# ScalarE's copies of the first phase of a fused SSM-convolution and gated-MLP gradient kernel: program order, and one deferrable copy per row block

## The chip, the core and the metric

The kernel runs on one core of a Trainium2 chip. A core has TensorE (matmuls, transposes; results go to PSUM), VectorE, ScalarE, GpSimd and SyncE, each with its own instruction stream in an order that is fixed when the kernel is built. SyncE, GpSimd and ScalarE also issue DMA transfers. The metric is device time in microseconds (us). The profiled execution is a single one, taken by the hardware profiler.

## The reference: what is computed

With S = 2048 rows, D = 1024 columns, F = 3584, all in bf16 at the edges:

```python
xn = layernorm(A_q)
k_shift = sum of four shifted copies of A_k times shift_k
kv = k_shift * A_v
y = irfft(rfft(kv padded to 2S) * rfft(ssm_k padded to 2S))[:S] + kv * ssm_D
s = xn * y
g = silu(((xn @ w_gate) * (xn @ w_up)) @ w_down)
out = A_q + s * g
```

The outputs are `out` and the gradients of all nine inputs for a given `grad_out`.

## The kernel before

**Phases.** In the first phase (about 31 to 505 us, with a start before it) TensorE computes the gate and up products. `F` is cut in 14 slabs of 256 columns (`wslab`, two buffers, loaded on SyncE's queue); the 2048 rows are 16 blocks of 128. A *row block*, or row, is one pass of `gu_unit`'s inner loop: eight matmuls of 128x512 (L671) into a PSUM tile `psg` (two buffers), then a ScalarE copy (L673, the *eviction*) to `gut` in SBUF. There are 14 x 16 = 224 rows; they are numbered 1 to 224 in order, and "eviction n" is that of row n. Four rows make a unit: its `gut` is stored to DRAM by a DMA on ScalarE's queue (L72), VectorE multiplies its halves to `hN` (three buffers, stored to `Hd` on GpSimd's queue), and of two units of `hN` 32 half transposes (`turn_pair`) make a PSUM tile `tr`, which two ScalarE copies (L705) bring to `hT`. `hT` has one buffer; SyncE stores it to `HTd` (L706), and the next pair's first copy must wait until that store has read it. `tr` has one buffer, which the filter transposes share.

Beside this, VectorE and TensorE run the forward long convolution, one step at a time, from a generator (`conv_forward`) that `tick` advances after each row. It handles eight blocks `ds` of 128 channels. For each one:

- the filter rows come from DRAM (`load_h`, GpSimd's queue, into half of `U5`), four ScalarE *quarter copies* reorder them into `hx` (L785, 128x512 each, read at a stride of eight elements), 32 half transposes turn them in `tr` (called at L807; the profile shows the helper's line, L565, for these and for those of `hN`), and two *back copies* bring them to `hx` again (L809);
- TensorE makes spectra in `psF` (PSUM, two buffers), and ScalarE copies them to `SP` (L256, L295; two buffers of two copies), which VectorE reads;
- VectorE sums, multiplies spectra and sums again; TensorE transforms back (`psI`, L455) and ScalarE copies to `yf` (L825).

For the first filter block TensorE transposes directly and two ScalarE copies scale into `hx` (L802). `turn_tables` makes the inverse tables `TI` by two copies of 128x2048 (L193).

After the first phase come the down product, the gating, and the backward products and convolutions, to 1914 us.

**What sets the order.** A planner orders each engine's instructions by its own estimate of when each is ready, with the program's order as priority. `keep_in_program_order` takes that freedom from an instruction: it stays behind all that was written before it on its engine. Before the change this holds for VectorE's steps (`tt`, `stt`) and the first matmul of each spectrum of `cmm`, not for ScalarE's copies. In the program, the four quarter copies stand at the first four steps of the spectral product and the turn at the fifth; both copies of a pair follow its transposes at once:

```python
for n, w in enumerate(product(KX, HX, KX, cs, False, 0)):
    if n < 4:
        h_order(ds + 1, n)
    else:
        h_turn(ds + 1)
    yield w
```

`pe_us` and `net` make a step of the convolution cheaper by the TensorE time that it added, so that the generator keeps pace with the rows.

Of the kernel before, what the change touches and what calls it, by code (L numbers as in the profile page):

```python
# [19 lines left out]
def build_kernel(  # L20
# [39 lines left out]
    def ld(out, in_):  # L60
        return nc.sync.dma_start(out=out, in_=in_)
# [9 lines left out]
    def sta(out, in_):  # L71
        return nc.scalar.dma_start(out=out, in_=in_)  # L72
# [113 lines left out]
    def turn_tables(psp):  # L186

        for j in range(2):
            ps = psp.tile([P, 8, 2, P], BF16, name="psT", tag="psF")
            for r in range(8):  # L190
                for k in range(2):
                    nc.tensor.transpose(ps[:, r, k, :], T4[j][:, r, k, :], ident[:])
            nc.scalar.copy(out=TI[:, j], in_=ps[:])  # L193
            yield


# [32 lines left out]
    def cmm(ps, T, x, rs, first=None, held=False):  # L229

        xr = x.rearrange("p (c r) d -> p r c d", c=2)
        for k in range(2):
# [5 lines left out]
            if first is not None and k == 0:  # L238
                nc.tensor.matmul(ps[:, 0, 0:P], T[:, 0, 0, :], first, start=False, stop=True)

    pe_us = [0.0]

    def net(w):
# [4 lines left out]
    def fwd4_half(x, i, wp, psp, first=None):  # L248

        pe_us[0] += 1.75  # L250
        SP = wp.tile([P, 2, 2, 512], F32, name="SP", bufs=2)
        for par in range(2):
            ps = psp.tile([P, 2, 2, 256], F32, name="psF")
            cmm(ps[:, 0], T4[par], x, (i, i + 4), first if i == 0 else None, True)
            cmm(ps[:, 1], T4[par], x, (i + 2, i + 6))
            nc.scalar.copy(out=SP[:, :, par], in_=ps[:].rearrange("p s k x -> p s (k x)"))  # L256
        return SP

    def fwd4_buf(wp):
# [27 lines left out]
    def fwd8_half(x, i, SP, psp, first=None, held=False):  # L287

        pe_us[0] += 0.87
        for j in range(2):  # L290
            r = 2 * i + j
            ps = psp.tile([P, 2, 2, 256], F32, name="psF")
            cmm(ps[:, 0], T4[0], x, (r,), first if r == 0 else None, held)
            cmm(ps[:, 1], T4[0], x, (r + 4,))
            nc.scalar.copy(out=SP[:, :, j], in_=ps[:].rearrange("p s k x -> p s (k x)"))  # L295

    def fwd8(SPs, X, W, C, ahead, late=False):

# [262 lines left out]
    def turn_halves(ps, src):  # L561

        for hh in range(2):
            rows = slice(64 * hh, 64 * hh + 64)
            ins = nc.tensor.transpose(ps(hh), src[rows], ident[rows, rows])  # L565
        return ins

    def halves(x):
        return x.rearrange("p b (h u) -> p h b u", h=2)
# [64 lines left out]
    later = []  # L634
    gu_mm = [None]

    def tr_tile():
        return ps_tr.tile([P, 2, 8, P], BF16, name="tr")

    def defer(fn):  # L640
# [14 lines left out]
    def gu_unit(sl, b0, n, w, tick):  # L655
# [11 lines left out]
        for i in range(n):  # L667
            q, qi = divmod(b0 + i, 4)
            ps = ps_gu.tile([P, 512], F32, name="psg")
            for dc in range(DC):  # L670
                gu_mm[0] = nc.tensor.matmul(ps[:], XNT[q][:, dc, qi * P:(qi + 1) * P],  # L671
                                            w[:, dc].rearrange("p a f -> p (a f)"), start=(dc == 0), stop=(dc == DC - 1))
            nc.scalar.copy(out=gut[:, :, i], in_=ps[:].rearrange("p (a f) -> p a f", a=2))  # L673
            flush(5)
            if i == 0:
                turn_late()
            hn[0]()
            hn[0] = nop
            tick()
        sta(GUd[sl, b0 // 8][:, :, b0 % 8:b0 % 8 + n], gut[:, :, 0:n])  # L680

        def multiply():
# [24 lines left out]

        def store(hT):
            half, rest = divmod(b0, 8)
# [30 lines left out]
    def conv_forward():  # L740
# [12 lines left out]
        def load_h(ds):  # L753
            hrow = U[5][:, 0:2048].rearrange("p (c u r) -> p c u r", c=2, r=8)
            cld(U[5][:, 0:2048], A_ssm_k[ds * P:(ds + 1) * P, :])
            S_["h", ds] = hrow
# [18 lines left out]
            yield 2.3  # L775

        def h_order(ds, part):
            if ds == 8:
                return
            hrow = S_["h", ds]  # L780
            if part == 0:
                S_["hx"] = cf.tile([P, NB, P], BF16, name="hx")
            if ds > 0:
                c, q = divmod(part, 2)
                nc.scalar.activation(S_["hx"][:, 4 * part:4 * part + 4, :], hrow[:, c, :, 4 * q:4 * q + 4].rearrange("p u r -> p r u"),  # L785
                                     ACT.Copy, scale=WSC)
                if part == 3 and ds + 1 < 8:
                    load_h(ds + 1)

        def h_turn(ds):  # L790
            if ds == 8:
                return
            hx = S_["hx"]
            pe_us[0] += 0.67
            if ds == 0:
                hrow = S_["h", 0]
                ps = tr_tile()
                for b in range(NB):
                    with tc.issue_after(tr_ln[0].ins) if b == 0 else nullcontext():
                        nc.tensor.transpose(ps[:, b // 8, b % 8, :], hrow[:, b // 8, :, b % 8], ident[:])  # L800
                    if b % 8 == 7:
                        nc.scalar.activation(hx[:, b - 7:b + 1, :], ps[:, b // 8], ACT.Copy, scale=WSC)  # L802
                load_h(1)
            else:
                ps = tr_tile()[:].rearrange("p h b x -> p h (b x)").rearrange("p h (b u) -> p h b u", u=64)
                for b in range(NB):
                    turn_halves(lambda hh: ps[:, hh, b], hx[:, b, :])  # L807
                for c in range(2):
                    nc.scalar.copy(out=halves(hx[:, 8 * c:8 * c + 8, :]), in_=ps[:, :, 8 * c:8 * c + 8])  # L809
            h_out.append(ds)  # L810

        def kvs(ds):
            return S_["kvt", ds // 2][:, :, ds % 2 * P:(ds % 2 + 1) * P]
# [1 line left out]
        def tail(ds):  # L815
            G = S_.pop(("G", ds))
            if ds < 7:
                yf = cs.tile([P, NB, P], BF16, name="yf")[:]
            else:
                yf = krow[:].rearrange("p a b d -> p (a b d)")[:, 0:NB * P].rearrange("p (b d) -> p b d", b=NB)  # L820
            for rq in range(2):
                ps = (ps_tr if cv_gone else ps_cv).tile([P, 4, 256], F32, name="psI", tag="tr" if cv_gone else "psF")
                inv_quad(G, ps, rq, ds in INV8)
                pe_us[0] += 0.9 if ds in INV8 else 1.8
                nc.scalar.copy(out=yf.rearrange("p (c r) d -> p r c d", c=2)[:, 4 * rq:4 * rq + 4], in_=rowps(ps))  # L825
# [50 lines left out]
        yield from shift(0)  # L876
        PIN[0] = True
        yield 3.9
        h_order(0, 0)
        h_turn(0)  # L880
        yield 0.1
        tl = turn_tables(ps_cv)
        sp = [half(0, S_["hx"], i, Dz[:, 0:P]) for i in range(2)]
        for ds in range(8):
# [11 lines left out]
            if ds == 0:  # L896
                yield from transform(0, 1, sp, HX, own_room(KX), lambda i: sph.append(half(0, kvs(0), i)), nop)
            else:
                yield from transform(ds, 0, sp, KX, own_room(HX), lambda i: sph.append(half(ds, S_["hx"], i, D0)), nop)
                S_["kst"] = st(KFd[ds], KX[:])  # L900
            calls = []

# [13 lines left out]
                S_["filters"] = False  # L916
            st(HFd[ds], HX[:])
            for n, w in enumerate(product(KX, HX, KX, cs, False, 0)):
                if n < 4:
                    h_order(ds + 1, n)  # L920
                else:
# [80 lines left out]
    def tick(by=1):  # L1002
        cnt[0] += by
        if cnt[0] == -4:
            pump((SHIFT_W + 4.05) / F_TOTAL)
        if cnt[0] >= -2:
            pump((SHIFT_W + (F_TOTAL - SHIFT_W) * (cnt[0] + 6.5) / (NT + 3.5)) / F_TOTAL)
# [60 lines left out]
    pss = [ps_bm.tile([P, D], F32, name="psbm") for i in range(2)]  # L1068
    with tc.issue_after(bm_first(range(4)).ins):
        flush()  # L1070
    for p_ in (ps_gu, fg, fw):
        p_.release()
    ub = pool("ub", 1, side="right")
# [752 lines left out]
```

## Time and profile before

| what | value |
|---|---|
| median of 3 runs | 1915.73 us (1915.4 to 1916.0) |
| profiled execution, its time | 1915.55 us |
| its span, first to last instruction | 1913.8 us |
| granted TensorE clock | 1.00 in all slices |
| first phase, 31 to 505 us: TensorE / VectorE / ScalarE busy | 463.15 / 462.48 / 307.15 us of 474 |
| eviction (L673), 128x512 | 0.59 us |
| spectra, back and `hT` copies, 1024 elements | 1.02 us |
| quarter copy (L785), 128x512 at a stride | 1.17 us |
| copy of `TI` (L193), 2048 elements | 1.86 us |

The profile gives each instruction its line in the kernel, its output and input tiles, its start and its duration. A number in square brackets in a timeline is the engine's idle time just ahead of the instruction, with what ended it. A matmul is shown for 0.38 us although the next may follow earlier, so TensorE counts as busy a little beyond what it issues. PE is TensorE, DVE VectorE, ACT ScalarE, SP SyncE; "ACTq" and "SPq" are the queues' DMA issues.

### The profile page before, as it was taken

Reading aid. Unit: us, or ns where it says so; the run is one execution under the profiler, and the core shown is the slowest. Engines: PE = TensorE matmul, PEld = TensorE weight load, DVE = VectorE, ACT = ScalarE, POOL = GpSimd, SP = SyncE. Lnnn points to the kernel's source line nnn. Section 1 sums busy time; section 2 is a strip of 40 time slices with the busy share of each in tenths; the row PEclk is TensorE's granted clock in tenths of the full one; section 3 lists DMA queues with packets and bytes.
Section 4 is the critical chain, followed back from the end, with each engine's and each line's share of the span. In section 5 each row is a group of like instructions: output and inputs, shape, how many; then the busy total and the mean of one; then the engine's idle time right before and its main releaser. Section 6 shows DMA issues by size and latency. Waiting matters only on the chain.

```text
span 1913.8 us, 28261 instructions
## 1 busy us (share of the span) xinstructions
PE 1890.4 (99%) x11350; PEld 1007.9 (53%) x11491; DVE 1550.6 (81%) x1711; ACT 664.0 (35%) x955; POOL 332.8 (17%) x465
## 2 busy tenths in 40 slices
PE   8999999999999999999999999999999999999999
PEld 5555555545544456666666665664444444444444
DVE  8999999999978556887999999999995205788862
ACT  5765666656433233432222222222222102110121
POOL 5121211201103220001031221111212101111120
PEclk9999999999999999999999999999999999999999
DMA  8777766769769997677887698585887999989862
GB/s 292 273 240 235 259 219 219 234 224 298 249 207 301 326 321 231 209 238 230 273 266 262 223 265 265 182 286 177 226 246 171 228 201 196 186 183 190 187 181 89
DMA packets 425107, 444.35 MB, mean 232 GB/s; under 512 B 268400, under 2 KB 342796, under 8 KB 410512
## 3 DMA queue, kind: packets, MB, share of 16 engines
q1 hardware_dynamic: 367504, 239.03, 46.4%
q0 software_dynamic: 41152, 174.15, 28.9%
q10 hardware_dynamic: 16320, 29.36, 4.1%
q8 instruction: 90, 1.47, 0.3%
q14 instruction: 41, 0.34, 0.1%
HBM read 193.87 MB, written 189.84 MB: 200 GB/s over the span
## 4 chain that ended last, share of the span: by engine, by line
PE 94%; DVE 2%; ACT 2%; issue 1%; DMA 0%; SPq 0%; ACTq 0%
PE psb L1517 20%; PE psx L1662 20%; PE psg L671 17%; PE psb L1500 10%; PE psbm L1052 10%; PE psb L1600 9%; PE psF L234 3%; PE tr L565 1%; PE psI L455 1%; DVE W L212 1%; ACT hx L785 1%; PE psY L1211 1%; PE psY L445 1%; PE psx L1600 1%; DVE bst L578 0%
## 5 line engine op out<-in xcount | busy, mean ns | idle before, releaser
L671 PE MATMUL psg<-wslab,U 128*128 128x512 bf16 x1727 | 398.0, 380 | 12.2 <-ACT gut L673 3.8
L1517 PE MATMUL psb<-U,U 128*128 128x512 bf16 x1792 | 397.1, 379 | 0.0
L1662 PE MATMUL psx<-U,dgut 128*128 128x512 bf16 x1505 | 331.0, 379 | 1.6
L1662 PEld LDWEIGHTS <-dgut 128*128 128x128 bf16 x1792 | 174.9, 98 | 211.8
L1517 PEld LDWEIGHTS <-U 128*128 128x128 bf16 x1792 | 174.9, 98 | 198.3
L671 PEld LDWEIGHTS <-U 128*128 128x128 bf16 x1792 | 172.0, 98 | 203.8 <-issue 9.8
L1500 PE MATMUL psb<-wdt,U 128*128 128x256 bf16 x1792 | 205.6, 273 | 0.0
L1500 PEld LDWEIGHTS <-U 128*128 128x128 bf16 x1792 | 174.8, 98 | 29.6
L212 DVE TENSOR_TENSOR W<-W 128x1024 f32<-128x1024 f32 (+1 forms) x189 | 186.5, 1003 | 4.0
L1600 PE MATMUL psb<-U,U 128*128 128x512 bf16 x797 | 176.1, 380 | 0.9
L1522 ACT CAST wb<-psb 128x512 bf16<-128x512 f32 x112 | 65.7, 587 | 315.3 <-PE psb L1517 307.5
L1267 DVE SCALAR_TENSOR_TENSOR dkp<-dkT,kT 128x1024 bf16<-128x1024 bf16 (+2 forms) x64 | 78.3, 1224 | 94.5 <-DMA dkT<-DKSHd 92.8
L1052 PE MATMUL psbm<-U,ht 128*128 128x512 bf16 x658 | 145.1, 379 | 0.7
L1600 PEld LDWEIGHTS <-U 128*128 128x128 bf16 x896 | 87.2, 98 | 104.5
L1694 ACT ACTIVATE dx_t<-dxn 128x1024 bf16<-128x1024 f32 x15 | 15.9, 1057 | 324.9 <-DVE dxn L212 320.1
L673 ACT CAST gut<-psg 128x512 bf16<-128x512 f32 x156 | 91.4, 592 | 101.9 <-PE psg L671 96.3
L1052 PEld LDWEIGHTS <-ht 128*128 128x128 bf16 x672 | 65.5, 98 | 78.3
L212 DVE TENSOR_TENSOR U<-U,dht 128x2048 bf16<-128x2048 bf16 x56 | 68.3, 1221 | 46.7 <-ACT dht L1502 46.7
L1502 ACT CAST dht<-psb 128x512 bf16<-128x512 f32 x112 | 65.7, 588 | 116.1 <-PE psb L1500 115.0
L66 POOL DMA_DIRECT2D Hd<-hN x54 | 37.1, 687 | 256.8 <-DVE hN L212 254.0
L1641 ACT CAST wbs<-psb 128x512 bf16<-128x512 f32 x51 | 29.9, 587 | 145.4 <-PE psb L1600 134.4
L212 DVE TENSOR_TENSOR W<-SP 128x1024 f32<-128x1024 f32 x64 | 74.3, 1219 | 1.5 <-ACT SP L295 0.8
(265 smaller groups left out, 2361.0 us busy)
## 6 DMA issues: line engine op xcount, KB each, us to landing
U<-GUd SPq DMA_DIRECT2D x28, 1024.0 KB, 9.2
DGd<-U SPq DMA_DIRECT2D x28, 1024.0 KB, 5.9
GUd<-gut ACTq DMA_DIRECT2D x39, 512.0 KB, 6.5
out_dram<-wb SPq DMA_DIRECT2D x112, 128.0 KB, 4.4
U<-Hd SPq DMA_DIRECT2D x14, 1024.0 KB, 5.9
Hd<-hN POOLq DMA_DIRECT2D x54, 256.0 KB, 4.4
HTd<-hT SPq DMA_DIRECT2D x24, 512.0 KB, 4.0
ht<-HTd SPq DMA_DIRECT2D x18, 512.0 KB, 7.8
```

Of the source, the lines that this page charges most:

```text
L212: pinned(V.tensor_tensor(o, a, b, op))
L234: mm = nc.tensor.matmul(ps[:, k].rearrange("p (c d) -> p c d", c=2), T[:, r, k, :], xr[:, r], start=(n == 0), stop=(n == len(rs) - 1 and ( ...
L671: gu_mm[0] = nc.tensor.matmul(ps[:], XNT[q][:, dc, qi * P:(qi + 1) * P], w[:, dc].rearrange("p a f -> p (a f)"), start=(dc == 0), stop=(dc ...
L673: nc.scalar.copy(out=gut[:, :, i], in_=ps[:].rearrange("p (a f) -> p a f", a=2))
L1052: mm = nc.tensor.matmul(ps[:, dh * 512:(dh + 1) * 512], ht(fc)[:, i * P:(i + 1) * P], WD[fc // 4][:, fc % 4, dh * 512:(dh + 1) * 512], sta ...
L1267: ins = V.scalar_tensor_tensor(prod[:].rearrange("p r d -> p (r d)")[:, lo:H], dkT[:, 0, lo:H], 1.0, kT[:, 0, 13 + m + lo:13 + m + H], op0 ...
L1500: nc.tensor.matmul(ps[:, x * SLW:(x + 1) * SLW], DBMT[2 * hf + g][:, dc, (b % 4) * P:(b % 4 + 1) * P], wdt[:, dc, :], start=(dc == 0), sto ...
L1502: nc.scalar.copy(out=dht[:, 2 * e:2 * e + 2].rearrange("p b f -> p (b f)"), in_=ps[:])
L1517: nc.tensor.matmul(ps[:], XN[b // 4][:, b % 4, dc * P:(dc + 1) * P], dgus[b // 8][:, :, b % 8], start=(b == 0), stop=(b == NB - 1))
L1522: nc.scalar.copy(out=wb[:, dc % 2].rearrange("p a f -> p (a f)"), in_=ps[:])
L1600: nc.tensor.matmul(ps, h[:, f, b, :], DBM[b // 4][:, b % 4, dh * 512:(dh + 1) * 512], start=(b == 0), stop=(b == NB - 1))
L1662: nc.tensor.matmul(ps[:, dh * 512:(dh + 1) * 512], t[n][:, f, i * P:(i + 1) * P], WGU[n][:, f, dh * 512:(dh + 1) * 512], start=(n == 0 and ...
```

## The change

Every ScalarE copy of the first phase that follows the start of the convolution (`PIN[0]`) is held in program order by `copied`; the pairs' and filters' deferrable copies too. These are no longer written where they arise. They go to a list, `slow`: four quarter copies, the turn and two back copies of a filter block at its end; the two copies of an `hT` at its head. `act_us` is a running account of ScalarE's work: `one_tick` takes 2.0 us off it for each row and adds 0.6 for the eviction, and each copy adds its cost. After each row `run_slow` takes entries while the account stays below 2.2. `tr_tile`, which hands out the single `tr` tile, first takes entries until the tile's copies are out; `hx(ds)` does so until the filter is there.

```diff
+    act_us = [0.0]
+    slow = []
+
+    def copied(us, ins=None):
+        act_us[0] += us
+        if ins is not None and PIN[0]:
+            tc.keep_in_program_order(ins)
+
+    def one_tick():
+        act_us[0] = max(0.0, act_us[0] - 2.0) + 0.6
+
+    def run_slow(all_=False):
+
+        while slow and (all_ or act_us[0] + slow[0][0] < 2.2):
+            us, fn = slow.pop(0)
+            copied(us)
+            fn()
...
-            nc.scalar.copy(out=SP[:, :, par], in_=ps[:].rearrange("p s k x -> p s (k x)"))
+            copied(1.0, nc.scalar.copy(out=SP[:, :, par], in_=ps[:].rearrange("p s k x -> p s (k x)")))
...
+    tr_held = []
+
     def tr_tile():
+        while tr_held:
+            slow.pop(0)[1]()
         return ps_tr.tile([P, 2, 8, P], BF16, name="tr")
...
-            nc.scalar.copy(out=gut[:, :, i], in_=ps[:].rearrange("p (a f) -> p a f", a=2))
+            one_tick()
+            copied(0.0, nc.scalar.copy(out=gut[:, :, i], in_=ps[:].rearrange("p (a f) -> p a f", a=2)))
...
             tick()
+            run_slow()
...
-            for g in range(2):
-                nc.scalar.copy(out=halves(hT[:, 2 * g:2 * g + 2].rearrange("p q a i s -> p (q a i) s")), in_=ps[:, :, 8 * g:8 * g + 8])
-            ht_st[0] = ld(to.rearrange("q f a s -> f q (a s)"), hT[:].rearrange("f q a i s -> f q (a i s)"))
+
+            def copy(g):
+                copied(0.0, nc.scalar.copy(out=halves(hT[:, 2 * g:2 * g + 2].rearrange("p q a i s -> p (q a i) s")),
+                                           in_=ps[:, :, 8 * g:8 * g + 8]))
+                if g == 1:
+                    tr_held.clear()
+                    ht_st[0] = ld(to.rearrange("q f a s -> f q (a s)"), hT[:].rearrange("f q a i s -> f q (a i s)"))
+            tr_held.append(True)
+            slow.insert(0, (1.0, lambda: copy(1)))
+            slow.insert(0, (1.0, lambda: copy(0)))
...
+        def h_back(ds, c):
+            copied(0.0, nc.scalar.copy(out=halves(S_["hx"][:, 8 * c:8 * c + 8, :]), in_=S_["hps"][:, :, 8 * c:8 * c + 8]))
+            if c == 1:
+                tr_held.clear()
+                h_out.append(ds)
+
+        def h_rows(ds):
+            if ds < 8:
+                pe_us[0] += 0.67
+                for part in range(4):
+                    slow.append((1.15, lambda part=part: h_order(ds, part)))
+                slow.append((0.0, lambda: h_turn(ds)))
+                for c in range(2):
+                    slow.append((1.0, lambda c=c: h_back(ds, c)))
...
+        def hx(ds):
+            while len(h_out) <= ds:
+                slow.pop(0)[1]()
+            return S_["hx"]
...
             for n, w in enumerate(product(KX, HX, KX, cs, False, 0)):
-                if n < 4:
-                    h_order(ds + 1, n)
-                else:
-                    h_turn(ds + 1)
+                if n == 1:
+                    h_rows(ds + 1)
                 yield w
...
     hn[0]()
+    run_slow(True)
```

The built orders, ScalarE's copies behind eviction n, and TensorE's work behind row n. S is a spectrum copy (on TensorE its matmuls), q a quarter copy, b a back copy (on TensorE the transposes of `hx`), T an `hT` copy (its transposes), I the table copy, Y a copy to `yf`, f the first filter's, t an early `hT` copy. A number behind a letter: so many matmuls of the next row come first.

```
row   ScalarE before / after    TensorE before / after
24    f       / f f             f           / f
25    -       / S S S S         -           / -
26    f SSSS t / t              f S6 t6 S7  / f S t S1 S3
41-43 q, qI, qq / -, I, -       -, I, -     / -, I, -
45-51 TT bb   / q T T q q q b   T46 b49     / T46 b50 b50+2
61-63 TT at 62 / T, T, T        T62         / T62
102   T T     / b b T           T           / - (T behind row 103, four matmuls of 104 first)
106-107 SSSSqq, qq / SSSS, -    S S1        / S S1
141-143 TT at 142 / T, T, T     T142        / T142+5
150   T T S S / b b T           T S         / - (six matmuls of S, T, the rest of S behind row 151)
157-159 qq, qqTTY, - / SS, -, Y Y158 T158   / S157 T158 Y159
192-194 SS, qqq, q / SS, -, T   S192        / S192
```

The last block of eight transposes of `hx` follows two matmuls of the next row at rows 50, 67, 99, 116 and 204, three at 147, five at 169; in each case the fourth quarter copy stands behind the eviction of that row. The orders of all engines after the first phase are the same in both kernels.

More of the change, by code (lines that the diff above doesn't have):

```diff
@@ L192, in turn_tables @@
                     nc.tensor.transpose(ps[:, r, k, :], T4[j][:, r, k, :], ident[:])
-            nc.scalar.copy(out=TI[:, j], in_=ps[:])
+            copied(1.9, nc.scalar.copy(out=TI[:, j], in_=ps[:]))
             yield
@@ L294, in fwd8_half @@
             cmm(ps[:, 1], T4[0], x, (r + 4,))
-            nc.scalar.copy(out=SP[:, :, j], in_=ps[:].rearrange("p s k x -> p s (k x)"))
+            copied(1.0, nc.scalar.copy(out=SP[:, :, j], in_=ps[:].rearrange("p s k x -> p s (k x)")))
     def fwd8(SPs, X, W, C, ahead, late=False):
@@ L777, in h_order @@
         def h_order(ds, part):
-            if ds == 8:
-                return
-            hrow = S_["h", ds]
             if part == 0:
                 S_["hx"] = cf.tile([P, NB, P], BF16, name="hx")
[L783 to L788, printed above, removed]
@@ L790, in h_turn @@
-        def h_turn(ds):
[L791 to L803, printed above, removed]
-            else:
-                ps = tr_tile()[:].rearrange("p h b x -> p h (b x)").rearrange("p h (b u) -> p h b u", u=64)
-                for b in range(NB):
-                    turn_halves(lambda hh: ps[:, hh, b], hx[:, b, :])
-                for c in range(2):
-                    nc.scalar.copy(out=halves(hx[:, 8 * c:8 * c + 8, :]), in_=ps[:, :, 8 * c:8 * c + 8])
-            h_out.append(ds)
+            c, q = divmod(part, 2)
@@ new lines, in h_order @@
+            copied(0.0, nc.scalar.activation(S_["hx"][:, 4 * part:4 * part + 4, :],
+                                             S_["h", ds][:, c, :, 4 * q:4 * q + 4].rearrange("p u r -> p r u"), ACT.Copy, scale=WSC))
+            if part == 3 and ds + 1 < 8:
+                load_h(ds + 1)
+        def h_turn(ds):
+            ps = tr_tile()[:].rearrange("p h b x -> p h (b x)").rearrange("p h (b u) -> p h b u", u=64)
+            for b in range(NB):
+                turn_halves(lambda hh: ps[:, hh, b], S_["hx"][:, b, :])
+            S_["hps"] = ps
+            tr_held.append(True)
@@ new lines, in h_first @@
+        def h_first():
+            hx = S_["hx"] = cf.tile([P, NB, P], BF16, name="hx")
+            hrow = S_["h", 0]
+            ps = tr_tile()
+            for b in range(NB):
+                with tc.issue_after(tr_ln[0].ins) if b == 0 else nullcontext():
+                    nc.tensor.transpose(ps[:, b // 8, b % 8, :], hrow[:, b // 8, :, b % 8], ident[:])
+                if b % 8 == 7:
+                    nc.scalar.activation(hx[:, b - 7:b + 1, :], ps[:, b // 8], ACT.Copy, scale=WSC)
+            load_h(1)
+            h_out.append(0)
@@ L824, in tail @@
                 pe_us[0] += 0.9 if ds in INV8 else 1.8
-                nc.scalar.copy(out=yf.rearrange("p (c r) d -> p r c d", c=2)[:, 4 * rq:4 * rq + 4], in_=rowps(ps))
+                copied(1.05, nc.scalar.copy(out=yf.rearrange("p (c r) d -> p r c d", c=2)[:, 4 * rq:4 * rq + 4], in_=rowps(ps)))
                 if ds == 7 and rq == 0:
@@ L878, in conv_forward @@
         yield 3.9
-        h_order(0, 0)
-        h_turn(0)
+        h_first()
         yield 0.1
@@ L898, in conv_forward @@
             else:
-                yield from transform(ds, 0, sp, KX, own_room(HX), lambda i: sph.append(half(ds, S_["hx"], i, D0)), nop)
+                yield from transform(ds, 0, sp, KX, own_room(HX), lambda i: sph.append(half(ds, hx(ds), i, D0)), nop)
                 S_["kst"] = st(KFd[ds], KX[:])
@@ L918, in conv_forward @@
             for n, w in enumerate(product(KX, HX, KX, cs, False, 0)):
-                if n < 4:
-                    h_order(ds + 1, n)
-                else:
-                    h_turn(ds + 1)
+                if n == 1:
+                    h_rows(ds + 1)
                 yield w
@@ L1070, in build_kernel @@
         flush()
+        run_slow(True)
     for p_ in (ps_gu, fg, fw):
```

## The prediction

> **What bounds the kernel now.** I read the page's first part, the busy time by stretch, TensorE's waits in the first phase, the timeline at the longest of them, and the tiles that the moved copies use.
>
> The page: TensorE is busy nearly always.
>
> ```profile
> span 1913.8 us, 28261 instructions
> ...
> PE 1890.4 (99%) x11350; PEld 1007.9 (53%) x11491; DVE 1550.6 (81%) x1711; ACT 664.0 (35%) x955; POOL 332.8 (17%) x465
> ```
>
> Busy time by stretch (TensorE, weight loads, VectorE, ScalarE, GpSimd). The idle time of the first phase (to 505 us) stands in a few short stretches. After 570 us there are 7 us of idle in 1344, and no gap of TensorE after 511 us exceeds 0.2 us: what the first phase loses or gains goes to the end undiminished.
>
> ```profile
> 100.00:125.00 25.00, 22.28 (x177) 11.35 (x179) 23.63 (x26) 16.27 (x21) 10.04 (x14) 1.00 0.78 259
> 125.00:250.00 125.00, 124.12 (x935) 68.35 (x950) 121.94 (x105) 78.81 (x105) 22.09 (x31) 1.00 0.74 243
> ...
> 365.00:380.00 15.00, 13.45 (x106) 7.52 (x105) 15.00 (x15) 12.94 (x17) 2.90 (x4) 1.00 0.52 175
> ...
> 570.00:1914.00 1344.00, 1336.59 (x7363) 713.21 (x7430) 1009.50 (x1125) 323.69 (x499) 225.50 (x310) 1.00 0.83 226
> ```
>
> Who holds TensorE in the first phase (waits, 31 to 505 us): ScalarE's evictions of `psg`, nothing else of size.
>
> ```profile
> engine line waited for: us in total, times, longest us
> PE psg L671 <- ACT gut L673: 3.8, 5, 1.5
> PE psg L671 <- ACT U L673: 2.5, 3, 1.4
> PE tr L565 <- DVE U L597: 0.7, 1, 0.7
> ```
>
> One such place (timeline, start and duration). A copy of filter rows (L785), the table copy (L193) and two more filter copies stand among the evictions; TensorE waits 0.45 and 1.39 us here, and 0.67 us at 111.73. These are rows 41 to 43 of the 224 row blocks, which I call rows.
>
> ```profile
> 105.28 0.57 ACT L673 CAST U<-psg 128x512 bf16<-128x512 f32 x1
> 105.75 1.14 ACT L785 ACTIVATE hx<-U 128x512 bf16<-128x512 bf16 x1
> 105.90 1.89 PE L671 MATMUL psg<-wslab,U 128*128 128x512 bf16 x8 [0.45 <-ACT U L673]
> ...
> 106.79 1.85 ACT L193 COPY TI<-psT 128x2048 bf16<-128x2048 bf16 x1
> ...
> 108.53 0.59 ACT L673 CAST U<-psg 128x512 bf16<-128x512 f32 x1
> 109.01 2.19 ACT L785 ACTIVATE hx<-U 128x512 bf16<-128x512 bf16 x2
> 109.17 1.89 PE L671 MATMUL psg<-wslab,U 128*128 128x512 bf16 x8 [1.39 <-ACT U L673]
> ```
>
> The tiles: quarter copies of `hx` take 1.16 us, twice an eviction of the same 128x512; a store of `hT` lands 3.7 us after its issue.
>
> ```profile
> L785 ACT ACTIVATE hx<-U x28: 1132/1164/1213, 104.2 to 446.0; 128x512 bf16<-128x512 bf16 x28
> ...
> DMA to landing us min/median/max: 2.1/3.7/8.5
> ```
>
> **The clock of one row.** Set 0 where TensorE has issued a row's last matmul. The 16 matmuls at 64.14 us take 3.62 us, the last one 0.38, so a matmul follows the other by 0.216 us and a row by 1.73. The eviction starts at 0.20 (67.60 to 67.79), the next ScalarE instruction 0.47 behind it (105.28 to 105.75), and TensorE starts 0.05 after the eviction it waits for ends (109.12 to 109.17). `psg` has two buffers: row n+2 needs eviction n. Copies of 1024 elements follow each other by 0.90 us, quarter copies by 1.05. A block of 32 half transposes costs 0.73: 32 at 0.0165 and about 0.10 at each end.
>
> **Removed: the pile-ups.** The six waits that the change takes apart are 0.45, 1.39 and 0.67 (rows 41 to 43), 0.38 (259.62 us, row 107), 1.50 (375.97, row 159) and 0.81 (446.17, row 194): 5.20. Each costs 0.16 more, since the last matmul is shown for 0.38 but the next could follow after 0.22: **-6.2 us**. In the new order no copies stand beside the table copy at row 42, behind the four spectra copies at row 106, at rows 157 and 158 or 193. The first wait of the view (0.94 us at 40 us) is not touched.
>
> **Added 1: transposes wait for the last quarter copy (rows 50, 67, 99, 116, 147, 169, 204).** Now the four quarter copies stand behind four evictions, and TensorE has 24 transposes straight after the row of the fourth, then two matmuls, then the last 8, which wait for it. The fourth is eviction 0.20, start 0.67, end 1.83, seen 1.88. TensorE is there at 0.10 + 24 x 0.0165 + 0.10 + 2 x 0.216 = 1.03. Wait 0.85 at 50, 99, 116 and 204; 0.89 at 67 (22 transposes); 0.77 at 147 (16, three matmuls); 0.20 at 169 (five matmuls): 5.3. Before, a turn started six rows or more behind its copies. The cut blocks add an end of 0.10 each seven times, and three more pieces (rows 66, 146, 210) 0.20 each: 1.3. **+6.6**. Bounds: the eviction's 0.59 in place of 1.16 gives waits of 0.28 and 3 us in all with the cuts; ScalarE a copy late gives 1.9 at each, 13. I take the row of the operation itself.
>
> [...]
>
> **Added 2: start of the filters (rows 24 to 27).** Both halves of `hx` (L802) now go before eviction 25, and TensorE's spectra matmuls straight after their transposes (E26 plus 0.49). The second copy runs 0.69 to 1.72 after row 26; TensorE stands from 0.49 to 1.77, 1.3 us; before, six matmuls of row 27 lay there. Then four spectra copies precede eviction 26, which ends 0.8 us after row 28 could start. Of these 2.1 I take off 0.36 (0.20 idle at 75.28 us plus the 0.16) and about 0.2 of smaller gaps that were there before: **+1.5**. Bounds: 0 if the copy is seen in time, 2.1 if nothing of the old waits was on the path.
>
> **Added 3: `hT` and its one buffer.** The second `hT` copy is put off to row 61 and to row 141, and the next pair forces the first of its own at 62 and 142. It must wait until the store has read `hT`. From row 61: copy ends 1.8, issued 1.83, landed 5.5 with the median 3.7; copy 62 runs 5.6 to 6.5 and eviction 63, pinned behind it, is out at 7.14. TensorE has rows 62, 63 and 64 and one block done at 6.04: 1.1 us. At 142 the block lies later: 1.2 us. Landing in 2.1 us makes both nothing, 8.5 us makes each 6. **+2.3**. Elsewhere three rows or more lie between, 5.2 us and more, which covers the median.
>
> **Added 4: forced flushes.** At row 102 two back copies and an `hT` copy stand before eviction 103: the back copies end at 2.7, transposes (begun at 2.75, due at 2.6) to 3.48, the copy to 4.3, the eviction out at 4.94, row 105 due at 4.34: 0.75 with the 0.15. At row 150 the tile is free 0.37 late; at 118 and 206 one back copy, and all is out before the row needs it. **+1.1**; 0 to 2.5.
>
> **At no cost:** the filter load on GpSimd's queue is issued up to 14 rows later, with 20 rows or more until its use, and the `Hd` stores behind it have three buffers of four rows each. On SP's queue slab loads and `HTd` stores change places; a slab is due 16 rows later, and a store held behind the slab's wait leaves six rows to the next pair. VectorE's steps move by one `hN` product; it lags 1 to 8 us behind the evictions, and TensorE, later than before, lets it catch up. Were TensorE earlier, VectorE (99% busy from 150 us) would soon be the bound. All orders after the first phase are the old ones.
>
> **Sum:** -6.2 + 6.6 + 1.5 + 2.3 + 1.1 = +5.3 us on the profiled 1915.55, 1920.9; the median of the runs lies 0.18 above the profiled one: **1921.0**.
>
> **Rivals.** (a) *Faster: the planner's arrival times hold on the chip.* It put the transposes and copies where it believes the operands arrive. For it: in the old order matmuls were laid six or seven behind `psF` copies and waited 0.17 us at most. Then the seven transposes, the two `hT` copies, the flushes and the start cost nothing, only the cuts' 1.3 stay: 1915.7 - 4.9 = 1910.8. It decides when all new waits together stay under 1.1 us. Against: no quarter copy or store was followed closely before. 0.14.
> (b) *A draw:* quarter copies behave like the eviction row (0.59), or the waits are partly covered: 6.6 becomes 3.0, the sum +1.7, 1917.4; with stores that land in 2.1 us also, 1915. 0.23.
> (c) *Stores land as at 116 or 156 us, beside slab loads (7.3 us):* 3.6 more twice, 1928. The slab loads are issued at rows 48, 64 and 144, so mostly not. 0.08.
> (d) *The change doesn't do what it says:* excluded; the orders are fixed when the kernel is built, and the new one stands as described.
>
> **Numbers.** The forecast has 0.55. Range: 1914.5 (most of b, none of a) to 1926.5 (sum with late ScalarE at some turns, or one late store). Alone, the forecast's range is 1919.5 to 1925. Two runs tell apart about 0.2%, 3.8 us. Slower by more: 0.55 + 0.08 = 0.63; within: 0.23; faster: 0.14.
>
> **What will show it.** The waits on `gut` and `U` at rows 41 to 43, 107, 159 and 194 gone; waits of transposes from `hx` on its copy in their place, 0.7 to 0.9 each, six times; ScalarE's `hT` waiting for a DMA twice; `psF` waiting some 1.3 us near 68 us; TensorE idle in 31 to 505 us up from 10.8 by about 4. I am wrong if the transposes don't wait, or if VectorE becomes what ScalarE's pinned spectra copies wait for.

## The result and the profile after

The changed kernel takes 1933.07 us (median of 4 runs, 1931.31 to 1934.82), the kernel before 1915.57 beside it (4 runs, 1915.08 to 1916.00). The ratio is 1.0092, its 95% interval 1.0076 to 1.0108: 17.5 us slower. The forecast was 1921.0 with a range to 1926.5: the side was right, the size was not.

Page of the kernel after, the span and the first part.

```profile
span 1933.1 us, 28394 instructions
...
PE 1904.4 (99%) x11491; PEld 1010.3 (52%) x11491; DVE 1550.7 (80%) x1711; ACT 667.2 (35%) x955; POOL 333.4 (17%) x465
```

The work is the same (the weight loads are 11491 in both; 141 matmuls are missing from the trace of the kernel before); the span has grown by 19.3 us. Busy time by stretch (TensorE, weight loads, VectorE, ScalarE, GpSimd, then TensorE's granted clock) says where: in the first phase, and at two places in it where the clock too has left 1.00. First the kernel before:

```profile
150.00:200.00 50.00, 49.64 (x369) 25.64 (x375) 49.52 (x37) 26.89 (x38) 6.38 (x9) 1.00 0.70 229
...
300.00:350.00 50.00, 49.63 (x401) 28.83 (x407) 49.38 (x44) 33.44 (x44) 12.98 (x18) 1.00 0.80 269
350.00:400.00 50.00, 48.19 (x336) 25.12 (x341) 49.66 (x47) 30.86 (x42) 6.42 (x10) 1.00 0.60 210
```

and the kernel after:

```profile
150.00:200.00 50.00, 45.38 (x328) 21.48 (x326) 43.33 (x31) 27.63 (x37) 6.86 (x10) 0.97 0.68 219
...
300.00:350.00 50.00, 46.27 (x350) 25.91 (x348) 49.55 (x40) 24.05 (x32) 12.51 (x17) 1.00 0.67 211
350.00:400.00 50.00, 46.76 (x331) 24.83 (x331) 40.60 (x40) 32.62 (x42) 5.68 (x8) 0.93 0.62 199
...
600.00:1933.00 1333.00, 1329.54 (x7383) 709.89 (x7381) 998.79 (x1107) 320.52 (x496) 220.36 (x301) 1.00 0.83 226
```

Waits of the kernel after, 31 to 530 us: first TensorE's, then the one of ScalarE that stands behind the largest.

```profile
PE psg L693 <- ACT gut L696: 12.2, 5, 6.2
PE tr L583 <- ACT hx L812: 4.2, 6, 0.7
PE psF L234 <- ACT hx L847: 1.1, 1, 1.1
PE tr L583 <- DVE U L615: 0.7, 1, 0.7
PE psg L693 <- ACT U L696: 0.6, 1, 0.6
...
ACT hT L730 <- DMA HTd<-hT: 16.8, 4, 8.2
```

The 2.5 us behind `U` are down to 0.6, seven transposes wait for the quarter copy (six of them over the bound of this view), and the evictions of `gut` now cost 12.2 where they cost 3.8. ScalarE itself waits 16.8 us for stores of `hT`. (L693 is the gate/up matmul, L696 its eviction, L812 the quarter copy, L583 the half transposes, L730 the `hT` copy.)

Timeline of the kernel after at four places: rows 41 to 43, the turn at row 50, and the two `hT` pairs of rows 62 and 142.

```profile
105.23 0.59 ACT L696 CAST U<-psg 128x512 bf16<-128x512 f32 x1 [1.14 <-PE psg L693]
...
106.12 1.87 ACT L193 COPY TI<-psT 128x2048 bf16<-128x2048 bf16 x1 [0.31 <-PE psT L192]
107.88 0.59 ACT L696 CAST U<-psg 128x512 bf16<-128x512 f32 x1
109.57 0.59 ACT L696 CAST U<-psg 128x512 bf16<-128x512 f32 x1 [1.10 <-PE psg L693]
...
120.51 0.52 PE L583 MATMUL tr<-ident,hx 64*128 64x64 bf16 x24
120.61 0.59 ACT L696 CAST gut<-psg 128x512 bf16<-128x512 f32 x1
...
121.09 1.13 ACT L812 ACTIVATE hx<-U 128x512 bf16<-128x512 bf16 x1
...
122.28 0.29 PE L583 MATMUL tr<-ident,hx 64*128 64x64 bf16 x8 [0.71 <-ACT hx L812]
...
152.90 0.56 POOL L66 DMA_DIRECT2D HFd<-HX  x1 [0.54 <-DVE HX L212]
153.44 1.16 POOL L66 DMA_DIRECT2D YFd<-yf  x1
154.07 0.37 SPq L61 DMA_DIRECT2D HTd<-hT  x1
160.69 1.01 ACT L730 COPY hT<-tr 128x1024 bf16<-128x1024 bf16 x1 [5.83 <-DMA HTd<-hT]
161.60 0.59 ACT L696 CAST gut<-psg 128x512 bf16<-128x512 f32 x1
...
162.24 5.30 PE L693 MATMUL psg<-wslab,U 128*128 128x512 bf16 x16 [3.88 <-ACT gut L696]
...
341.45 0.57 POOL L66 DMA_DIRECT2D HFd<-HX  x1 [1.31 <-DVE HX L212]
341.97 0.37 SPq L61 DMA_DIRECT2D HTd<-hT  x1
...
350.96 1.01 ACT L730 COPY hT<-tr 128x1024 bf16<-128x1024 bf16 x1 [8.20 <-DMA HTd<-hT]
352.51 6.01 PE L693 MATMUL psg<-wslab,U 128*128 128x512 bf16 x16 [6.24 <-ACT gut L696]
```

The pile-up beside the table copy is gone: the two evictions behind it come without a wait of TensorE. At row 50 the last eight transposes stand 0.71 us for the copy that began at 121.09. At row 62 the store of `hT` was issued at 154.07, and the copy that needs the tile runs at 160.69; the eviction is pinned behind that copy, and TensorE behind the eviction. At row 142 the same takes from 341.97 to 350.96. Beside both stores stand the 1 MB store `HFd` and, issued at 153.44 and 339.01, the 0.5 MB store `YFd`. By the packets they do not weigh alike: at row 62 the `hT` store moves once those of `HFd` run out, near 157 us, and `YFd` begins only at 158.33, when four fifths of it are through; at row 142 all of `YFd` goes first, then `HFd` shares with it until 348 us.

What the profile gives for each term of the sum, from start to start of the matmuls, less the 0.216 us in which one follows the other:

| term | predicted us | found us |
|---|---|---|
| pile-ups removed (rows 41 to 43, 107, 159, 194) | -6.2 | none of them is left |
| turns wait for the last quarter copy | 5.3 | 0.87, 0.91, 0.87, 0.88, 0.77, 0.26, 0.88: 5.4 |
| cut blocks | 1.3 | not told apart |
| start of the filters | 1.3 + 0.8, less 0.6 | 1.27 + 0.81; 0.36 there before: 1.7 |
| `hT` at rows 62 and 142 | 1.1 + 1.2 | 4.04 + 6.41: 10.5 |
| `hT` at row 94 | 0 | 0.68 |
| flushes at rows 102 and 150 | 0.75 + 0.37 | 0.79 + 0.29 |
| halved clock | not there | 4.1 |

The clock: the trace has TensorE's granted clock at 0.5 for 3.41 us from 162.84 and for 6.83 us from 350.57. Matmuls there follow each other by 0.427 us in place of 0.216. Half of the working time in it is lost: 3.41 / 2 = 1.7 and, as TensorE starts again only at 352.51, (357.40 - 352.51) / 2 = 2.45. With the cuts at their predicted 1.3 the column gives -6.2 + 5.4 + 1.3 + 1.7 + 10.5 + 0.7 + 1.1 + 4.1 = +18.6 of the 19.3 by which the span grew.

### The profile page after: what moved, and what is told of

The parts are those of the page before. It is cut to its first block, busy times and chain, and to the rows that moved or that the text cites. A ratio compares the mean times of both kernels' runs of the same rounds, so it can differ in the third digit from the quotient of the medians.

```text
span 1933.1 us, 28394 instructions
## 1 busy us (share of the span) xinstructions
PE 1904.4 (99%) x11491; PEld 1010.3 (52%) x11491; DVE 1550.7 (80%) x1711; ACT 667.2 (35%) x955; POOL 333.4 (17%) x465
## 4 chain that ended last, share of the span: by engine, by line
PE 95%; ACT 2%; DMA 2%; DVE 1%; SPq 0%; issue 0%; ACTq 0%
PE psx L1705 20%; PE psb L1560 20%; PE psg L693 18%; PE psb L1543 10%; PE psbm L1094 10%; PE psb L1643 9%; PE psF L234 3%; DMA HTd<-hT 1%; PE psI L473 1%; PE tr L583 1%; PE psY L1254 1%; PE psY L463 1%; PE psx L1643 1%; DVE bst L596 0%; DMA wslab<-in_B_w_gate_dram 0%; ACT hx L812 0%
## 5 line engine op out<-in xcount | busy, mean ns | idle before, releaser
L693 PE MATMUL psg<-wslab,U 128*128 128x512 bf16 x1792 | 408.8, 382 | 16.2 <-ACT gut L696 12.2
L693 PEld LDWEIGHTS <-U 128*128 128x128 bf16 x1792 | 172.4, 98 | 212.0 <-issue 23.9
L696 ACT CAST gut<-psg 128x512 bf16<-128x512 f32 x156 | 91.8, 590 | 99.3 <-PE psg L693 95.8
```

The lines of the kernel that those rows point to most:

```text
L696: copied(0.0, nc.scalar.copy(out=gut[:, :, i], in_=ps[:].rearrange("p (a f) -> p a f", a=2)))
```

## The experiments

My theory at this point: the deferred `hT` copies cost 14.6 us (waits and clock), the turns 5.4, and program order itself next to nothing. Rivals: the order as such (an engine held behind each copy that waits); VectorE, 99% busy, would take back any gain; the clock's fall has another reason.

**Without program order.** `copied` keeps its account and its deferrals, but pins nothing:

```
     def copied(us, ins=None):
         act_us[0] += us
-        if ins is not None and PIN[0]:
-            tc.keep_in_program_order(ins)
```

> The changed kernel without the pins: copies are still deferred in the program by the account, but the planner may order them. The built order then has the quarter copies in bunches again (rows 41 to 43, 57, 85 to 87, 106, 135 to 137, 157, 193) and the turns six rows behind, nearly as in the kernel before. Theory A: the old pile-ups return, all new waits go: 1915.6 us, within 2 us. Rival D (the deferral in the program is itself what costs, by later transposes, stores and loads): 1922 or more.

Measured: 1915.67 us, ratio 1.0004 (0.9995 to 1.0013). Its waits behind `gut` and `U` are 3.6 and 2.6 us: the pile-ups of before are back. The deferrals alone do nothing that can be measured; ScalarE's order is the planner's.

**Program order without deferrals.** The kernel before, with the copies of ScalarE pinned that the change pins, and none put off:

```
-            nc.scalar.copy(out=TI[:, j], in_=ps[:])
+            pin_act(nc.scalar.copy(out=TI[:, j], in_=ps[:]))
...
             for g in range(2):
-                nc.scalar.copy(out=halves(hT[...]), in_=ps[:, :, 8 * g:8 * g + 8])
+                pin_act(nc.scalar.copy(out=halves(hT[...]), in_=ps[:, :, 8 * g:8 * g + 8]))
```

> The kernel before, with the first phase's ScalarE copies held in program order and none of them put off: one of the two parts of the change alone. My theory, that the loss lies with the copies that were put off next to work that needs them and not with program order as such: the 6.2 us removed, against 1.5 at the start and about 0.8 twice where a pair of hT copies now stands ahead of an eviction, so about 1912.4 us (1910.5 to 1915). Rival, that program order itself is the loss (an in-order engine held behind each copy that waits): 1925 us or more.

Measured: 1912.87 us, ratio 0.9988 (0.9979 to 0.9997). Program order is not the loss; alone it is a small gain. TensorE's new waits are the two at the start (1.27 and 0.81), 0.56 at 226 and 0.69 at 387 us. So the 20 us between this kernel and the changed one come with the deferrals, once they are pinned.

**Filling the idle time.** 12 and 22 matmuls whose results nobody reads go into the waits of rows 62 and 142. The waits stay, the idle time in them doesn't.

```
+            rown[0] += 1
+            if rown[0] in (64, 144):
+                with tc.issue_after(gu_mm[0].ins):
+                    fill = ps_cv.tile([P, 2, 2, 256], F32, name="psF")
+                    for _ in range(12 if rown[0] == 64 else 22):
+                        nc.tensor.matmul(fill[:, 0]..., ident[:], w[:, 0]..., start=True, stop=True)
```

> The changed kernel, with 12 matmuls of 128x512 behind row 64 and 22 behind row 144 into a spectra tile that nobody reads (2.6 and 4.8 us), where TensorE waits 3.9 and 6.2 us; the outputs are not touched. The waits as such stay: the evictions come when they came. Theory A with the clock as a cost of its own: the granted clock stays at 1.0, and 1.7 + 2.4 = 4.1 us come back, 1929.0 us. Rival C (the lower clock costs nothing, because it falls into the wait): 1933, unchanged.

Measured: 1929.18 us, 3.9 less than the changed kernel; the clock is 1.0 throughout, where idle stretches of 1.22 and 1.41 us are left. So 4 us of the loss are the clock's, and here the clock falls with the idle time, 3.88 and 6.24 us in the changed kernel.

**The two stores four rows earlier.** The pairs of rows 54 and 134 are flushed at rows 58 and 138; nothing else is moved by hand (TensorE's order and that of SyncE's transfers shift a little beside it).

```
             tick()
             run_slow()
+            rown[0] += 1
+            while rown[0] in (58, 138) and tr_held:
+                slow.pop(0)[1]()
```

> The changed kernel, with the second hT copy of the pairs of rows 54 and 134 brought out at rows 58 and 138 instead of 61 and 141; nothing else is moved by hand. Theory A (the loss is the sum of separate waits of TensorE, each behind a ScalarE copy; the two waits for the hT store are 4.0 and 6.4 us of it, and the clock that is halved for 3.4 and 6.8 us after them 4.1 more): -14.6 us against the changed kernel, up to 1 given back where the store still lands late, so about 1919 us (1918 to 1921). Rival B (VectorE, which waits 23 us for evictions and spectra in the changed kernel, sets the pace; TensorE would wait for it next): less than 5 us come back, 1928 or more.

Measured: 1918.94 us, ratio 1.002 (1.0011 to 1.003), 14.1 less than the changed kernel; the two waits and the clock had 10.5 + 4.1 = 14.6 to give. No wait of TensorE at rows 62 and 142 is left. The profiled execution took 1924.25, since TensorE stood 3.92 us at 1611 us, far behind the edit, and ran at half its clock after it (mean clock 0.999, in the eight others 1.000); the eight others lie within 1918.15 and 1919.76, and the median of all nine hardly depends on that one.

**The turn a row later.** The turn enters the list of slow work with a cost, so that it comes a row behind the last quarter copy.

```
-                slow.append((0.0, lambda: h_turn(ds)))
+                slow.append((0.5, lambda: h_turn(ds)))
```

> The changed kernel, with the turn of a filter block entered at a cost of 0.5 instead of 0, so that it is taken one row behind the fourth quarter copy. Theory A: the seven waits of transposes for that copy (0.87, 0.91, 0.87, 0.88, 0.77, 0.26, 0.88: 5.4 us) and their cuts (about 1) go: -6.4 us, 1926.7 us. Rival B: nothing comes back, since VectorE sets the pace: 1932 to 1934.

Measured: 1925.39 us, ratio 1.0055 (1.004 to 1.007): 7.7 less than the changed kernel, a little more than the 6.4 expected. No transpose waits for a quarter copy. But that the total came so near is in part luck. By the trace TensorE's work has moved against the stores, so that row 62 waits 4.44 us (0.4 more) and row 142 only 2.55 (3.9 less), the half clock costs 3.4 in place of 4.1, and about 2 us of small waits are new at 320, 366 and 520 us. That leaves, as an estimate, some 5.5 us for the turns with their cuts.

**All three mended.** Both edits above, and pins only from the first block's first transform on.

```
-        if ins is not None and PIN[0]:
+        if ins is not None and PIN_ACT[0]:
...
                 S_["kst"] = st(KFd[0], KX[:])
+                PIN_ACT[0] = True
```

> The changed kernel with three things mended together: the two late pairs of half transposes flushed four rows earlier (at rows 58 and 138), the turn of a filter queued one row behind its last quarter copy, and ScalarE's copies held in program order only from the first block's first transform on, so that the start is the one of before. My theory, that the loss is the sum of the waits named (start 1.5, turns 5.4, hT and the halved clock 14.5): only the 6.2 us that the change removes, less 0.7 at row 94 and 0.8 at row 102, remain, so about 1911 us (1910 to 1913). Rival B, that TensorE gains nothing because VectorE (99% busy from 150 us) sets the pace as soon as ScalarE doesn't: 1914 us or more, with waits for VectorE's tiles in their place.

Measured: 1913.14 us, ratio 0.999 (0.9981 to 0.9999): 0.1 above the range that my theory gave, and below the rival's 1914. The named waits make up nearly all of the loss; what is left over are 0.83 and 0.79 at rows 94 and 102, 0.59 behind a spectra copy and one wait of 1.22 us for VectorE at 507, so that the rival has a small part.

**Only the quarter copies held.** Pins on the quarter copies alone, the `hT` pairs copied at once, the turn a row later.

```
     def copied(us, ins=None):
         act_us[0] += us
-        if ins is not None and PIN[0]:
-            tc.keep_in_program_order(ins)
...
-            tr_held.append(True)
-            slow.insert(0, (1.0, lambda: copy(1)))
-            slow.insert(0, (1.0, lambda: copy(0)))
+            for g in range(2):
+                copied(1.0)
+                copy(g)
...
-            copied(0.0, nc.scalar.activation(S_["hx"][:, 4 * part:4 * part + 4, :],
+            tc.keep_in_program_order(nc.scalar.activation(S_["hx"][:, 4 * part:4 * part + 4, :],
...
-                slow.append((0.0, lambda: h_turn(ds)))
+                slow.append((0.5, lambda: h_turn(ds)))
```

> The changed kernel with only the quarter copies of the filters held in place (one a row), the hT pairs copied at once, and the turn of a filter queued one row behind its last quarter copy; all other ScalarE copies are left to the planner. My theory, that the pile-ups of the kernel before come from quarter copies that were bunched: the 6.2 us go and no new wait comes, so about 1909.4 us (1908.5 to 1912). Rival B, that VectorE sets the pace as soon as ScalarE doesn't: 1914 us or more.

Measured: 1911.17 us, ratio 0.998 (0.9972 to 0.9989): the fastest of all here, and faster than both kernels. Its page and its waits of TensorE, 31 to 530 us:

```profile
span 1909.3 us, 28406 instructions
...
PE 1896.8 (99%) x11491; PEld 1009.0 (53%) x11491; DVE 1550.2 (81%) x1711; ACT 666.8 (35%) x955; POOL 334.5 (18%) x465
...
PE psg L692 <- ACT gut L695: 1.5, 2, 0.9
PE tr L582 <- DVE U L614: 0.7, 1, 0.7
PE tr L752 <- ACT hT L754: 0.6, 1, 0.6
PE tr L582 <- DVE hN L212: 0.5, 1, 0.5
PE psF L234 <- ACT SP L273: 0.4, 1, 0.4
```

The bunched quarter copies were the pile-ups: with them one a row all six are gone, and 0.5 for VectorE's `hN`, 0.4 for a spectra copy and 0.5 more at a `gut` at 471 us are what came next. VectorE does take something back, but 0.5 us, not all.

**The large stores apart.** Why do the two `hT` stores land so late? First, `HFd` of every block, and `YFd` of all but the last (its lines are left out here), are held back on GpSimd's queue until behind the next `Hd` store:

```
...
-            st(HFd[ds], HX[:])
+            S_["late"].append(lambda: st(HFd[ds], HX[:]))
             for n, w in enumerate(product(KX, HX, KX, cs, False, 0)):
...
+                if n == 4:
+                    while S_["late"]:
+                        tc.keep_in_program_order(S_["late"].pop(0)())
```

> The changed kernel, with the two large stores of the convolution (HFd, 1 MB, and YFd, 0.5 MB) held back on GpSimd's queue until behind the Hd store after rows 62 and 142, so that they no longer stand beside the hT store that the next hT copy waits for. ScalarE's and TensorE's orders are those of the changed kernel. My theory, that these two stores are what made the hT store land 6.5 and 8.9 us after its issue: the waits at rows 62 and 142 fall to about 1.1 to 1.5 each and the clock stays at 1.0, so about 1921 us (1920 to 1923.5). Rival, that the hT store lands late for other reasons (loads of k and v and of slabs): both waits stay above 3.5 us and the time at 1929 us or more; between these, row 142 alone stays long, some 1925.5 us.

Measured: 1943.51 us, ratio 1.0149 (1.0135 to 1.0163), far from the 1921 expected. At row 62 the wait fell as the theory had it, but to 2.55 us and not to 1.5; at row 142 it stayed at 5.50; and row 94 went from 0.68 to 5.10. The timeline of this kernel there:

```profile
224.31 13.95 SPq L61 DMA_DIRECT2D HTd<-hT  x2
...
231.21 1.28 POOL L66 DMA_DIRECT2D YFd<-yf  x1
232.26 0.78 POOL L66 DMA_DIRECT2D HFd<-HX  x1
...
235.45 1.01 ACT L730 COPY hT<-tr 128x1024 bf16<-128x1024 bf16 x1 [6.90 <-DMA HTd<-hT]
...
237.00 3.57 PE L693 MATMUL psg<-wslab,U 128*128 128x512 bf16 x8 [4.94 <-ACT gut L696]
```

The edit had moved the crowd, not removed it. With the stores out of their way the loads of `k` and `v` came earlier, beside the `hT` stores of rows 94 and 142, and the held stores ended up beside the one of row 94, which lands after 11.06 us in place of 6.63. Held stores also make TensorE wait for spectra copies at 139, 520 and 522 us (1.49, 1.97 and 0.48), and the clock is halved for 6.83 us twice. So this run suggests that neighbours decide the landing, but is no test of row 142.

**The same at two places alone.** `HFd` and `YFd` (again left out here) are held back at rows 62 and 142 only, and the loads that follow the latter wait for them. The order of GpSimd's queue is all that differs from the changed kernel.

```
...
-            st(HFd[ds], HX[:])
+            if ds in (1, 4):
+                S_["late"].append(lambda: st(HFd[ds], HX[:]))
+            else:
+                st(HFd[ds], HX[:])
...
+                if n == 4:
+                    while S_["late"]:
+                        S_["kst"] = S_["late"].pop(0)()
+                        tc.keep_in_program_order(S_["kst"])
```

> The changed kernel with the large stores and loads on GpSimd's queue moved at two places alone: the HFd store (1 MB) and the YFd store (0.5 MB) that stood beside the hT stores of rows 62 and 142 are issued after them, and the loads of k and v near row 142 after these. All other engines run the changed kernel's order, and the hT store of row 94 keeps its neighbours. My theory, that what moves beside the hT store decides how late it lands: the wait at row 62 is 2.5 us as with all stores apart, the one at row 142 falls from 6.4 to 1.2 to 2.5, row 94 stays at 0.7, the clock stays at 1.0: 1923 us (1921.5 to 1925). Rival, that the hT store lands late for its own sake at row 142: its wait stays above 4.5 us, the clock is halved behind it, and the time is 1928 us or more.

Measured: 1922.05 us, ratio 1.0033 (1.0021 to 1.0044), 11.0 less than the changed kernel. Its timeline:

```profile
152.71 0.37 SPq L61 DMA_DIRECT2D HTd<-hT  x1
...
157.57 1.01 ACT L730 COPY hT<-tr 128x1024 bf16<-128x1024 bf16 x1 [4.07 <-DMA HTd<-hT]
...
159.12 3.23 PE L693 MATMUL psg<-wslab,U 128*128 128x512 bf16 x9 [2.11 <-ACT gut L696]
...
338.92 0.37 SPq L61 DMA_DIRECT2D HTd<-hT  x1
...
341.92 1.01 ACT L730 COPY hT<-tr 128x1024 bf16<-128x1024 bf16 x1 [2.22 <-DMA HTd<-hT]
...
343.48 3.61 PE L693 MATMUL psg<-wslab,U 128*128 128x512 bf16 x16 [0.26 <-ACT gut L696]
```

At row 142 the store lands after 2.91 us in place of 8.89 and costs 0.42 in place of 6.41 (1.2 to 2.5 were expected); at row 62 it lands after 4.76 in place of 6.52 and costs 2.27 in place of 4.04; row 94 keeps its 0.73. The two waits and the clock had 6.0 + 1.8 + 4.1 = 11.9 to give, of which 11.0 came back. That settles it: what moves beside the `hT` store sets most of its landing, and its landing sets the loss. In the profiled execution the clock is still halved once, behind 2.11 us of idle time at row 62; the four runs of seven in which it stays at 1.0 take 1921.6 to 1922.1, the others 1923.4 to 1925.7.

**Shorter packets beside it.** `HFd` goes out in packets of 4 KB, as the trace has them (the edit was laid out for 2), in place of 8:

```
-    HFd = dram.tile([8, P, 16, 256], BF16, name="HFd")
+    HFd = dram.tile([8, 4, P, 4, 256], BF16, name="HFd")
...
-            st(HFd[ds], HX[:])
+            st(HFd[ds].rearrange("c p a x -> p c a x"), HX[:].rearrange("p (c a) x -> p c a x", c=4))
```

> The changed kernel with the HFd store in packets of 2 KB in place of 8 KB (another layout of the scratch tensor HFd in memory, and its loads later in the program likewise); nothing is moved. In the trace of the changed kernel the hT store (packets of 1 KB) near 345 us moves about as many packets as the stores beside it, and so an eighth of their bytes. My theory, that queues take turns by packets: there the hT store gets a third in place of a ninth and lands 1.5 to 2 us sooner; the wait at row 142 falls from 6.4 to about 4.5 us and the halved clock behind it gets shorter, row 62 (where the hT store moves nothing until the 8 KB packets are through) stays at about 4: 1930.5 us (1929 to 1931.5). Rival, that only the bytes in front count: both waits as before, 1933 us; the loads in shorter packets may add to either.

Measured: 1935.82 us, ratio 1.0109 (1.0086 to 1.0133), not to be told from the changed kernel, and a miss against 1930.5. The queues' packets from 345 to 347 us, in the changed kernel (q1 is the `hT` store):

```profile
q0 software_dynamic: 88, 0.70, 89.7%
q1 hardware_dynamic: 86, 0.09, 13.4%
```

and with the edit:

```profile
q0 software_dynamic: 146, 0.60, 81.8%
q1 hardware_dynamic: 143, 0.15, 21.3%
```

The theory holds in this stretch: packet for packet, 88 to 86 and 146 to 143, so that the `hT` store with its 1 KB packets moves 0.09 MB beside 0.70, an eighth of the others' bytes, or 0.15 beside 0.60, a quarter. Its worth was misjudged: the store of row 142 lands after 8.51 us in place of 8.89, the one of row 62 after 7.38 in place of 6.52. At row 142 no packet of it moves for the first 2.5 to 2.8 us in either kernel, and 300 to 400 of its 512 move only after 347.5 us, when the bytes of `HFd` are nearly through. The waits are 6.03 and 4.89.

A second buffer for `hT`, the direct cure, was not tried; it would take 4 KB a partition.

## Why the prediction was right in its sign and wrong in its size

- **Removed, right.** None of the six waits came back in the new order. The kernel that keeps only this part's effect gains 4.0 us against the 1915.17 beside it, as some 2 us of new small waits stand against the 6.2.
- **Added 1, right:** 5.4 us of waits where 5.3 were worked out from the quarter copy's own row; the turn a row later takes them away.
- **Added 2, right:** 1.27 and 0.81 where 1.3 and 0.8 stood.
- **Added 4, right:** 0.79 and 0.29 where 0.75 and 0.37 stood.
- **Added 3 failed.** Mechanism and places were right, the size was not: 10.5 us at rows 62 and 142 for 2.3. The step took "landed 5.5 with the median 3.7", a median over stores of which most have few neighbours. These two landed after 6.52 and 8.89. Put into the prediction's own chain these give 1.1 + 2.8 = 3.9 and 1.2 + 5.2 = 6.4, against 4.04 and 6.41 found: the landing is all that was wrong in it. The bound was in the text ("8.5 us makes each 6"), and rival (c), a late landing, came nearest with 1928, but it was priced at 0.08 because slab loads are not issued there. The neighbours that matter were others, `HFd` and `YFd` on GpSimd's queue and the loads behind them, and the prediction did not lay out which transfers stand beside the two stores. The trace of before had a warning at the place: its `hT` stores issued at 156.44 and 334.40 us landed after 7.28 and 5.95. "Three rows or more", said to cover the median elsewhere, failed at row 94, where the store landed after 6.63: 0.68.
- **A term was missing: the clock.** Before, no wait of TensorE in the first phase exceeded 1.5 us and the clock stood at 1.00, so the sum had no price for a longer one. It cost 4.1 us here, and 3.9 came back when the idle time was filled. With the 8.2 us that Added 3 lacked, the 0.7 of row 94 and these 4.1, the forecast's 1921 becomes 1934; 1933.07 was measured.
- Rivals (a) and (b) fell: the seven transposes did wait, and the quarter copy they waited for took 1.13 us and not 0.59. That VectorE becomes the bound fell too: 1911.17 was reached with 0.5 us behind VectorE. Of the signs named, TensorE's idle time from 31 to 505 us missed: it rose from 10.8 to 19.2 us, not by about 4.

## What to carry to other kernels

A copy that is put off into a fixed order carries its tile with it: before deferring one, ask when its buffer is needed next, and lay out who is on the DMA queues while the store behind it moves. A median landing time is a price only for a store with median neighbours; read the landing at the place, or bound it with the worst row there. To break up a pile-up, hold in place only the few instructions that bunch: that was 0.2% faster here, the full order alone 0.1% faster, and the full order with deferrals 0.9% slower.

## What the runs showed of the hardware

**The clock of two traces changed in steps of 3.41 us.** In the trace of the changed kernel it stands in stretches of 157.01 us (at 1.00), 3.41 (0.5), 184.32 (1.00), 6.83 (0.5) and 1576.96 (1.00), in that of the kernel before in one of 1908.05 (1.00): 46, 1, 54, 2, 462 and 559 times 3.4133. Laid on steps of that length, the step that ends with the fall at 162.84 us has 2.82 us of TensorE's idle time, and the one that ends with the fall at 350.57 is idle throughout. Of the halved steps the first behind 350.57 still has 1.94 us of idle time, and a second follows it; that second one and the one behind 162.84 have none, and 1.00 follows. Every other step, up to the ends of the programs, has at most 1.18 us in the changed kernel and 1.53 in the kernel before, and no fall comes behind it. So in these two traces 1.53 us inside a step was not followed by a fall and 2.82 was; where between them it begins they do not show. The length of a wait alone does not tell. One of 2.16 us at 8.20 us in the changed kernel lies across the edge of two steps, which have 1.14 and 1.12 us of idle time, and no fall came. Behind 2.11 us (two places clear) the weight loads follow each other by 0.43 us, at half the clock, and behind 2.39 us (large stores apart) 16 matmuls take 3.61 us and the clock is 1.00 from 150 to 200 us.

**Two queues moved about as many packets each, not bytes,** from 345 to 347 us, as the pairs 88 to 86 (changed kernel) and 146 to 143 (shorter packets) above show. But a store may move nothing at all for a while. From the issue of row 62's store to 156.4 us the changed kernel's queues moved

```profile
q0 software_dynamic: 112, 0.92, 104.7%
```

and no packet of q1: its first came 2.7 us after the issue, when the 8 KB packets of `HFd` had nearly run out. At row 142 it came 2.8 us after, when the 4 KB packets of `YFd` had nearly run out. With nothing beside it, the first packet of row 62's store came 0.9 us after (large stores apart). Why it came so late at rows 62 and 142 is open.

**A store can have a slow tail.** With nothing beside it, the store of row 62 still took 4.8 us (two places clear) and 5.0 (large stores apart), that of row 142 took 2.9 (two places clear). In the first of these, nearly all of the store was through within 2.5 us; from 155.0 to 157.4 us (two places clear) the GB/s in 40 equal slices were

```profile
GB/s 393 222 120 17 0 17 0 17 0 17 0 17 0 17 17 17 17 34 17 17 34 17 34 17 17 34 17 34 17 34 17 17 34 17 0 0 0 0 0 0
```

a trickle of single packets. Beside its 512 packets of 1 KB, a store of `hT` has 16 of 4 bytes. For row 62 in the changed kernel the last of the 16 ended 1.37 us behind the one before it, and beside the store a 16 KB packet of a queue that the profile calls "instruction" began at 158.13 us and took 0.96 us (1.75 with the large stores apart). From 140 us on, the traces of the kernel before and of the changed kernel have 34 `hT` stores whose 4-byte packets can all be counted. Of these, 10 had such a packet (8 or 16 KB) beside them, and their last 4-byte packet ended 0.70 us behind the one before it in the median (0.00 to 1.98); for the 24 without, it was 0.03 us (0.00 to 0.94). So packets of that queue go with the tail, though not store by store; why is not shown, and no run changed them.
